# Retention, four experts and a Mish layer: product 4 ahead of product 3, and the border between the two layers re-ordered

## The chip, the cores and the metric

The kernel runs on one core of a Trainium2 chip. The metric is the device time of one execution in microseconds, as the median of several runs. Engines are named as the profile names them: PE (TensorE, matrix products), ACT (ScalarE), DVE (VectorE), POOL (GpSimd), SP (SyncE, which issues the DMAs).

## What is computed

Retention over q, k, v gives x (1152 tokens, 512 wide); four experts of width 1024 with ReLU and a weight per token follow, then one layer of width 2048 with Mish.

```python
scores = scale * np.matmul(q, k.transpose(0, 1, 3, 2))
attn = np.matmul(scores * Dmat[None], v)
x = attn.transpose(0, 2, 1, 3).reshape(1152, 512)
p = domain_probs / (domain_probs.sum(-1, keepdims=True) + 1e-09)
out = 0
for e in range(4):
    out += p[:, e:e + 1] * (np.maximum(x @ w1[e], 0.0) @ w2[e])
h = out @ w_in
g = h * np.tanh(np.log1p(np.exp(np.minimum(h, 20.0))))
return g @ w_out
```

## The kernel before, in words

**Arithmetic.** Every fp32 operand is kept as two fp32r parts, a rounded high part (made by an ACT copy) and a remainder (a subtraction on DVE or POOL). A product of two operands is three matmuls: high by remainder, high by high, remainder by high. A "product" of the first weights below is six matmuls of 512 columns (two depth blocks), all at L226.

**Units.** The hidden width of both layers is cut into 12 units of 512: units 0 to 7 belong to the four experts (NE is 8), units 8 to 11 to the Mish layer. The 1024 first tokens are multiplied with w1 by a seven-product scheme (PRODUCTS): P1 to P7 use sums of weights (key G, made on POOL at L135 to L138) and differences T1 to T4 of x. The four PSUM banks b00, b01, b10 and b11 of a call hold P1+P2, P7+P4, P5+P3 and P6. The last 128 tokens go a direct way, with x in xc.

**Steps.** `steps()` writes the order of the program as a list, and `feed_forward` emits it; every engine keeps that order. S (u, c) is `first_pair`: seven products for half c of unit u. L is `first_last`: the last tokens' product with w1 (12 matmuls, L677), turned over through DRAM (`turn_blocks`, `turn_rest`). Y (u, c, tb) is `second`: one w2 product of 24 matmuls (L693; in the Mish layer `second_t`, L709). T is the last tokens' w2 product (12 matmuls, L709). In a usual unit the order is S, L (c = 0); Y, Y (tb = 1 of the unit before); T; S, L (c = 1); Y, Y (tb = 0). Between units 7 and 8, where the result of the experts becomes the new x, it is Y, Y (tb = 0), T, Y, Y (tb = 1), S (8, 0), L (8, 1), S (8, 1).

**Inside S.** The products run as 1, 5, 7, 6, 2, 3, 4, and in the first pair of units 0 and 8 as 1, 5, 2, 3, 7, 6, 4. P1, P5 and P7 are copied out by ACT (`copy_sum`); POOL adds them into p5 (L636, L637); DVE makes p16 from P6 and P1, adds p16 to P3 and P4 and p5 to P6 (all at L622). `hidden` turns a finished bank into h: an ACT ReLU (L609) and a DVE remainder (L610), or in the Mish layer two ACT operations (L605, L606) and a DVE remainder (L607). The first two blocks of a pair's h (P2 and P4) are those for tb = 0, the others (P3 and P6) for tb = 1.

```python
            if n in (3, 6) and 3 in done and 6 in done:
                add(done[3], done[3], p16)
                add(done[6], done[6], p5)
                hidden(u, h[1][:, :, 0], done[3])
                hidden(u, h[1][:, :, 1], done[6])
```

**Lists inside S.** `early` is run behind P5, `later` behind P7: there stand weight tasks and float64 steps that were put off.

**Weights.** `weight_task` takes the next entry of a list: weight sums on POOL, or a split of a 512 KB weight tile (`split_w`: ACT copy L159, POOL remainder L163 in four pieces). A split whose tile PE still reads waits for PE.

**Float64.** The Mish layer's weights come as float64. While the experts run, each half tile goes through four stages (`STAGES`): `exponents64` (two DVE operations), `range64` (four ACT operations), `values64` (three DVE operations, then the next load, `load64`), `store64` (to DRAM). `turn64` moves each half under way by one stage per step other than S, and starts a new one at every Y of units 0 to 6 and 8.

**Border.** `new_x` splits each finished block of the experts' output into x and makes the differences T1 to T4 (L732, L742, L743; splits at L203 and L204).

Of the kernel before, what the change touches and what calls it, by code (L numbers as in the profile page):

```python
# [51 lines left out]
def steps():  # L52

    seq = [("S", 0, 0), ("L", 0, 1), ("S", 0, 1)]
    for u in range(NU):
        nxt = u + 1 < NU
        border = u == NE - 1
        seq += [("Y", u, c, 0) for c in range(2)]  # L60
        if nxt and not border:
            seq += [("S", u + 1, 0), ("L", u + 1, 0)]
        if border:
            seq.append(("T", u))
        seq += [("Y", u, c, 1) for c in range(2)]
        if not border:
            seq.append(("T", u))
        if border:
            seq += [("S", u + 1, 0), ("L", u + 1, 1), ("S", u + 1, 1)]
        elif nxt:  # L70
            seq += [("S", u + 1, 1), ("L", u + 1, 1)]
    return seq
# [7 lines left out]
def retention_moe_mish(ctx: ExitStack, tc: tile.TileContext, kq_in, kv_in, probs, w1, w2, w64, cdec, out):  # L80
# [643 lines left out]
    def new_x(c, tb, a):  # L724

        b11, b12, b21, b22 = (
            acc[:, ks, ts] for ks in (slice(0, 2), slice(2, 4)) for ts in (slice(0, TB), slice(TB, 2 * TB))
        )

        def difference(out, x, y):  # L730

            dve.tensor_tensor(out=y, in0=x, in1=y, op=ALU.subtract)  # L732
            split_x(xop[:, :, out], y, dve)

        if (c, tb) != (0, 1):
            split_x(xop[:, :, {(0, 0): B11, (1, 0): B21, (1, 1): B22}[c, tb]], a, pool)
        if (c, tb) == (0, 1):
            difference(T1, b12, b11)
        elif (c, tb) == (1, 1):
            difference(T3, b22, b12)  # L740

            dve.tensor_tensor(out=b11, in0=b22, in1=b11, op=ALU.subtract)  # L742
# [146 lines left out]
```

## Time and profile before

| what | value |
|---|---|
| runs | 659.39 us median of 3 (658.25 to 661.88) |
| the profiled execution | 661.8 us, of which the span of its instructions is 659.7 us |
| PE busy | 614.9 us (93%), 3183 matmuls |
| DVE, ACT, POOL busy | 64%, 47%, 60% |
| granted PE clock | 0.975 of 2.4 GHz on average |
| chain that ended last | PE 35%, POOL 24%, DVE 14%, ACT 12%, issue 10%, DMA 4% |

PE stands near its work for the whole span, so a stretch in which it waits is time that the kernel could lose; a wait of another engine costs only where PE waits behind it. A row of the timeline merges instructions of one kind that follow each other: start, length, line, tiles (out<-in), count, and in brackets the idle time of the engine before it with what ended it.

### The profile page before, as it was taken

Reading aid. Unit: us, or ns where it says so; the run is one execution under the profiler, and the core shown is the slowest. Engines: PE = TensorE matmul, PEld = TensorE weight load, DVE = VectorE, ACT = ScalarE, POOL = GpSimd, SP = SyncE. Lnnn points to the kernel's source line nnn. Section 1 sums busy time; section 2 is a strip of 40 time slices with the busy share of each in tenths; the row PEclk is TensorE's granted clock in tenths of the full one; section 3 lists DMA queues with packets and bytes.
Section 4 is the critical chain, followed back from the end, with each engine's and each line's share of the span. In section 5 each row is a group of like instructions: output and inputs, shape, how many; then the busy total and the mean of one; then the engine's idle time right before and its main releaser. Section 6 shows DMA issues by size and latency. Waiting matters only on the chain.

```text
span 659.7 us, 8578 instructions
## 1 busy us (share of the span) xinstructions
PE 614.9 (93%) x3183; PEld 504.4 (76%) x3183; DVE 423.6 (64%) x570; ACT 309.7 (47%) x478; POOL 395.9 (60%) x455
## 2 busy tenths in 40 slices
PE   7999999999999999999999999785769989999997
PEld 7977788788788788788787787574658868878886
DVE  2896665877887887877787787565334954244242
ACT  2665366356356346446447437213545644335130
POOL 2677849847747847747747847805951684663400
PEclk7999999999999999999999999896989989999999
DMA  8932315434424424524523523420210233121022
GB/s 332 380 102 83 107 49 155 119 125 140 144 84 144 129 95 159 139 76 136 155 97 133 159 88 104 128 64 32 61 68 2 97 86 105 35 50 43 1 64 112
DMA packets 56513, 72.30 MB, mean 110 GB/s; under 512 B 31128, under 2 KB 38296, under 8 KB 56472
## 3 DMA queue, kind: packets, MB, share of 16 engines
q1 hardware_dynamic: 56472, 71.76, 34.0%
q8 instruction: 25, 0.41, 0.2%
q14 instruction: 16, 0.13, 0.1%
HBM read 57.57 MB, written 14.17 MB: 109 GB/s over the span
## 4 chain that ended last, share of the span: by engine, by line
PE 35%; POOL 24%; DVE 14%; ACT 12%; issue 10%; DMA 4%; SPq 1%; POOLq 0%; DVEq 0%; ACTq 0%
POOL w L163 14%; PE ps L709 13%; PE b L226 11%; PE ps L693 7%; DVE b L622 3%; DVE h L610 3%; ACT h L609 3%; POOL p L636 2%; POOL p L637 2%; POOL wr L136 1%; POOL wr L137 1%; DMA O<-g 1%; POOL wr L135 1%; POOL wr L138 1%; ACT e L559 1%
## 5 line engine op out<-in xcount | busy, mean ns | idle before, releaser
L163 POOL TENSOR_TENSOR w<-wr,w 128x256 fp32r<-128x256 f32 x288 | 236.0, 851 | 154.7 <-ACT w L159 154.7
L226 PE MATMUL b<-x,w 128*128 128x512 f32 x1008 | 241.9, 397 | 4.8 <-DVE h L607 3.7
L226 PEld LDWEIGHTS b<-x,w 128*128 128x128 f32 x1008 | 188.9, 188 | 52.3 <-DVE h L607 4.5
L693 PE MATMUL ps<-h,w 128*128 128x512 f32 x768 | 179.3, 391 | 10.7 <-DVE h L610 10.7
L693 PEld LDWEIGHTS ps<-h,w 128*128 128x128 f32 x768 | 142.6, 188 | 42.9 <-DVE h L610 14.1
L709 PE MATMUL ps<-w,h 128*128 128x512 f32 x384 | 93.2, 401 | 7.2 <-ACT h L606 7.1
L709 PEld LDWEIGHTS ps<-w,h 128*128 128x128 f32 x384 | 73.3, 194 | 25.0 <-issue 8.6
L159 ACT ACTIVATE w<-wr 128x1024 fp32r<-128x1024 f32 x72 | 74.4, 1049 | 19.5 <-POOL wr L138 14.6
L238 ACT ACTIVATE p<-b 128x512 f32<-128x512 f32 x72 | 40.9, 593 | 58.4 <-PE b L226 58.3
L610 DVE SCALAR_TENSOR_TENSOR h<-b,h 128x512 fp32r<-128x512 f32 x64 | 43.4, 688 | 36.4 <-ACT h L609 35.3
L609 ACT ACTIVATE h<-b 128x512 fp32r<-128x512 f32 x64 | 38.0, 593 | 57.7 <-DVE b L622 56.6
L622 DVE TENSOR_TENSOR b<-b,p 128x512 f32<-128x512 f32 x72 | 48.5, 691 | 12.8 <-POOL p L637 12.7
L636 POOL TENSOR_TENSOR p<-p,p 128x512 f32<-128x512 f32 x24 | 31.1, 1295 | 37.5 <-ACT p L238 37.4
L607 DVE TENSOR_TENSOR h<-b,h 128x512 fp32r<-128x512 f32 x32 | 22.1, 691 | 44.7 <-ACT h L606 44.7
L677 PE MATMUL ps<-w,xc 128*128 128x256 f32 x288 | 39.1, 286 | 10.5 <-DVE xc L204 9.6
L677 PEld LDWEIGHTS ps<-w,xc 128*128 128x128 f32 x288 | 38.2, 194 | 13.2 <-issue 10.0
L558 ACT ACTIVATE e<-e,cbias 128x512 uint32<-128x512 uint32 x32 | 23.0, 720 | 52.0 <-DVE e L546 52.0
L756 DVE TENSOR_TENSOR ps<-ps,pb 128x1024 f32<-128x1024 f32 x28 | 34.3, 1226 | 15.4 <-PE ps L693 15.4
L780 DVE TENSOR_TENSOR acc<-acc,ps 128x1024 f32<-128x1024 f32 (+1 forms) x15 | 16.7, 1115 | 39.2 <-PE ps L709 39.2
L709 PE MATMUL ps<-w,hl 128*128 128x512 f32 x144 | 37.1, 410 | 4.2 <-ACT hl L609 4.2
L709 PEld LDWEIGHTS ps<-w,hl 128*128 128x128 f32 x144 | 28.4, 199 | 10.9 <-ACT hl L609 4.6
L622 DVE TENSOR_TENSOR p<-b,p 128x512 f32<-128x512 f32 x24 | 16.5, 686 | 30.0 <-PE b L226 19.0
(80 smaller groups left out, 624.3 us busy)
## 6 DMA issues: line engine op xcount, KB each, us to landing
wr<-w SPq DMA_DIRECT2D x32, 512.0 KB, 4.2
w<-w SPq DMA_DIRECT2D x32, 512.0 KB, 3.8
kq<-kq_in SPq DMA_DIRECT2D x8, 576.0 KB, 8.1
O<-g SPq DMA_DIRECT2D x16, 256.0 KB, 4.4
W<-g SPq DMA_DIRECT2D x16, 256.0 KB, 3.3
wr<-O SPq DMA_DIRECT2D x8, 512.0 KB, 3.3
wr<-W SPq DMA_DIRECT2D x8, 512.0 KB, 4.4
kv<-kv_in SPq DMA_DIRECT2D x7, 544.0 KB, 8.5
```

The source lines that it names most:

```text
L159: act.activation(out=w[:, 0], in_=t, func=AF.Copy)
L163: lo_engine.tensor_tensor(out=w[:, 1, k], in0=t[:, k], in1=f32(w[:, 0, k]), op=ALU.subtract)
L226: pe.matmul(o[t][j], w[:, a, 2 * kh + kk, fb * P:(fb + 1) * P], xop[:, b, r, kk], start=opens and kk == 0 and i == 0, stop=kk == 1 and i == 2,
L238: act.activation(out=t, in_=src, func=AF.Copy)
L609: act.activation(out=out[:, 0], in_=src, func=AF.Relu)
L610: dve.scalar_tensor_tensor(out=out[:, 1], in0=src, scalar=0.0, in1=f32(out[:, 0]), op0=ALU.max, op1=ALU.subtract)
L622: dve.tensor_tensor(out=out, in0=a, in1=b, op=ALU.add)
L636: pool.tensor_tensor(out=p5, in0=p5, in1=p7, op=ALU.add)
L677: pe.matmul(o, xc[:, b, k], w[:, a, k], start=k == 0 and n == 0, stop=k == 3 and n == 2)
L693: pe.matmul(o[:, j], w[:, a, d:d + P], h[:, b, f], start=i == f == n == 0, stop=i == f == 1 and n == 2,)
L709: pe.matmul(o[:, n], h, w[:, b, f * DM:(f + 1) * DM], start=k == f == i == 0, stop=k == f == 1 and i == 2,)
L756: dve.tensor_tensor(out=o, in0=o, in1=pbb, op=ALU.mult)
```

## The change

The order of the products in a usual S becomes 1, 5, 7, 6, 2, 4, 3, and the sums and hidden blocks of P3 and P6 are made when all seven products are done, so behind P4's. `early` becomes `behind`, a table from a product's number to what is emitted behind it. In the first pairs of units 0 and 8 the last tokens' product stands behind P2 instead of P5. At the border, T stands between the last two Y; T1 is made right behind it, and the differences for T3 and T2 are taken behind P1 ahead of the split of xc, the rest (`last_t`) behind P5. New float64 halves start at L and at the Y of c = 0 (not in unit 7), the weight task of a step stands ahead of its float64 stages, the last Y of unit 7 has none, and the Y of unit 8 have two. The float64 tiles have five buffers instead of four. The first load of q and k is issued as two halves, by SP and by ACT. `cbias` has 16 columns instead of 3.

```diff
     for u in range(NU):
...
+        y = [[("Y", u, c, tb) for c in range(2)] for tb in range(2)]
+        t = [("T", u)]
+        if u == NE - 1:
+            seq += y[0] + y[1][:1] + t + y[1][1:] + [("S", u + 1, 0), ("L", u + 1, 1), ("S", u + 1, 1)]
...
-    cbias = keep.tile([P, 3], F32, tag="cbias", name="cbias")
+    cbias = keep.tile([P, 16], F32, tag="cbias", name="cbias")
...
-            sp.dma_start(out=kq, in_=kq_in[b, pr])
+            if u == 0:
+                sp.dma_start(out=kr, in_=kq_in[b, pr, :, 0])
+                act.dma_start(out=qr, in_=kq_in[b, pr, :, 1])
+            else:
+                sp.dma_start(out=kq, in_=kq_in[b, pr])
...
-            if n in (3, 6) and 3 in done and 6 in done:
+            for f in behind.get(n, ()):
+                f()
+            if len(done) == 7:
                 add(done[3], done[3], p16)
                 add(done[6], done[6], p5)
...
+    def last_x():
+
+        x_split(B22, b22, pool)
+        x_minus(b12, b22, b12)
+        x_minus(b11, b22, b11)
+        split_x(xc, acc_last, dve)
+
+    def last_t():
+        x_split(T3, b12)
+        x_minus(b21, b21, b11)
+        x_split(T2, b11)
+        x_split(T4, b21)
...
                 turn_rest(acc_last)
+                x_minus(b11, b12, b11)
+                x_split(T1, b11)
...
-                if (u, c) == (NE, 0):
-                    early.insert(0, lambda: split_x(xc, acc_last, dve))
-                if (u, c) in ((0, 0), (NE, 0)):
-                    early.append(lambda: first_last(u, 0))
+                late = (u, c) in ((0, 0), (NE, 0))
+                behind = {}
+                if late:
+                    behind[2] = [lambda: first_last(u, 0)]
+                    behind[5] = early if u == 0 else [last_t]
+                if (u, c) == (NE, 0):
+                    behind[1] = [last_x]
...
-                first_pair(u, c, early, later, (1, 5, 2, 3, 7, 6, 4) if late else (1, 5, 7, 6, 2, 3, 4))
+                first_pair(u, c, behind, later, (1, 5, 2, 3, 7, 6, 4) if late else (1, 5, 7, 6, 2, 4, 3))
...
+            if m != "S" and (m, u, *at) != ("Y", NE - 1, 1, 1):
+                task(2 if u in (0, NE) and m == "Y" else 1)
             if m != "S":
-                turn64(m == "Y" and u != NE - 1, later.append if ahead else lambda f: f())
+                new = (m, *at) in (("L", 0), ("L", 1), ("Y", 0, 0), ("Y", 0, 1)) and not i_x <= i <= i_x + 7 and i > 2
+                turn64(new, later.append if ahead else lambda f: f())
...
-            if m != "S":
-                task(2 if u == 0 and m == "Y" else 1)
```

In the changed file the lines from L198 on stand at most 8 away from those of before: L620 and L608 there are L622 and L610 here, L603 and L604 are L605 and L606, L153 is L159, L232 is L238, L198 is L204, L755, L756 and L769 are L756, L757 and L770, L660 is L662.

DVE at unit 2, c = 1 (S (2, 1)), before: b00 is P2's bank, b01 P4's, b10 P3's, b11 P6's.

```order
L622 TENSOR_TENSOR p16_1661<-b11_1616,p1_1625 128x512
L610 SCALAR_TENSOR_TENSOR h_1617<-b00_1613,h_1617 128x512
L622 TENSOR_TENSOR b10_1615<-b10_1615,p16_1661 128x512
L622 TENSOR_TENSOR b11_1616<-b11_1616,p5_1633 128x512
L610 SCALAR_TENSOR_TENSOR h_1618<-b10_1615,h_1618 128x512
L610 SCALAR_TENSOR_TENSOR h_1618<-b11_1616,h_1618 128x512
L622 TENSOR_TENSOR b01_1614<-b01_1614,p16_1661 128x512
L610 SCALAR_TENSOR_TENSOR h_1617<-b01_1614,h_1617 128x512
```

And now:

```order
L620 TENSOR_TENSOR p16_1656<-b11_1615,p1_1624 128x512
L608 SCALAR_TENSOR_TENSOR h_1616<-b00_1612,h_1616 128x512
L620 TENSOR_TENSOR b01_1613<-b01_1613,p16_1656 128x512
L608 SCALAR_TENSOR_TENSOR h_1616<-b01_1613,h_1616 128x512
L620 TENSOR_TENSOR b10_1614<-b10_1614,p16_1656 128x512
L620 TENSOR_TENSOR b11_1615<-b11_1615,p5_1632 128x512
L608 SCALAR_TENSOR_TENSOR h_1617<-b10_1614,h_1617 128x512
L608 SCALAR_TENSOR_TENSOR h_1617<-b11_1615,h_1617 128x512
```

P4's sum and remainder (b01) moved from the end to the third and fourth place, ahead of the two sums of P3 and P6, of which the latter reads POOL's p5.

DVE between units 7 and 8, before, from the turning over of the last tokens on (acc holds the experts' output, x and xc are the new operands, ps is a w2 product):

```order
L662 STREAM_TRANSPOSE hs_697<-acc_87 128x128 x4
L756 TENSOR_TENSOR ps_3848<-ps_3848,pb_3314 128x1024
L757 TENSOR_TENSOR acc_87<-acc_87,ps_3848 128x2x512
L732 TENSOR_TENSOR acc_87<-acc_87 128x2x512
L204 TENSOR_TENSOR x_84<-acc_87,x_84 128x1024
L756 TENSOR_TENSOR ps_3878<-ps_3878,pb_3314 128x1024
L757 TENSOR_TENSOR acc_87<-acc_87,ps_3878 128x2x512
L732 TENSOR_TENSOR acc_87<-acc_87 128x2x512
L204 TENSOR_TENSOR x_84<-acc_87,x_84 128x1024
L742 TENSOR_TENSOR acc_87<-acc_87 128x2x512
L743 TENSOR_TENSOR acc_87<-acc_87 128x2x512
L204 TENSOR_TENSOR xc_85<-acc_87,xc_85 128x512
```

And now, from the last tokens' sum on:

```order
L769 SCALAR_TENSOR_TENSOR acc_87<-ps_3853,pl_86,acc_87 128x4x128
L660 STREAM_TRANSPOSE hs_698<-acc_87 128x128 x4
L727 TENSOR_TENSOR acc_87<-acc_87 128x2x512
L198 TENSOR_TENSOR x_84<-acc_87,x_84 128x1024
L755 TENSOR_TENSOR ps_3879<-ps_3879,pb_3309 128x1024
L756 TENSOR_TENSOR acc_87<-acc_87,ps_3879 128x2x512
L727 TENSOR_TENSOR acc_87<-acc_87 128x2x512 x2
L198 TENSOR_TENSOR xc_85<-acc_87,xc_85 128x512
L198 TENSOR_TENSOR x_84<-acc_87,x_84 128x1024
L727 TENSOR_TENSOR acc_87<-acc_87 128x2x512
```

The last tokens' sum and turning over stand ahead of the last w2 product's sums instead of ahead of two products' sums; T1's difference and remainder follow them, and xc's remainder has one x remainder ahead of it instead of two.

ACT from unit 8's first pair into its second, before (w is a weight copy, p1, p5 and p7 the copied products):

```order
L605 ACTIVATE b10_3920<-b10_3920 128x512
L606 ACTIVATE h_3923<-b10_3920 128x512
L605 ACTIVATE b11_3921<-b11_3921 128x512
L606 ACTIVATE h_3923<-b11_3921 128x512
L605 ACTIVATE b01_3919<-b01_3919 128x512
L606 ACTIVATE h_3922<-b01_3919 128x512
L238 ACTIVATE p1_4062<-b00_4050 128x512
L238 ACTIVATE p5_4070<-b10_4052 128x512
L238 ACTIVATE p7_4078<-b01_4051 128x512
L159 ACTIVATE w_4082<-wr_3846 128x1024
L159 ACTIVATE w_4088<-wr_4023 128x1024
L605 ACTIVATE b00_4050<-b00_4050 128x512
```

And now:

```order
L603 ACTIVATE b01_3907<-b01_3907 128x512
L604 ACTIVATE h_3910<-b01_3907 128x512
L603 ACTIVATE b10_3908<-b10_3908 128x512
L604 ACTIVATE h_3911<-b10_3908 128x512
L603 ACTIVATE b11_3909<-b11_3909 128x512
L604 ACTIVATE h_3911<-b11_3909 128x512
L153 ACTIVATE w_4039<-wr_3823 128x1024
L232 ACTIVATE p1_4059<-b00_4047 128x512
L232 ACTIVATE p5_4067<-b10_4049 128x512
L232 ACTIVATE p7_4075<-b01_4048 128x512
L603 ACTIVATE b00_4047<-b00_4047 128x512
L604 ACTIVATE h_4051<-b00_4047 128x512
```

P4's bank (b01) is first of the three; the two weight copies between p7 and the first Mish of the second pair are gone, and one stands ahead of p1.

## Rows read from the trace of the kernel before

**Rows 1.** Waits of all engines: engine, line, releaser: us in total, times, longest.
```profile
PE ps L693 <- DVE h L610: 10.7, 8, 1.6
...
DVE e L546 <- DMA w<-w: 6.0, 6, 2.6
```

**Rows 2.** PE timeline, units 2 and 3: start us, us, engine, line, [idle before].
```profile
163.72 3.57 PE L693 MATMUL ps<-h,w 128*128 128x512 f32 x15
168.80 7.78 PE L693 MATMUL ps<-h,w 128*128 128x512 f32 x33 [1.51 <-DVE h L610]
176.42 9.96 PE L226 MATMUL b<-x,w 128*128 128x512 f32 x42
...
187.62 11.05 PE L693 MATMUL ps<-h,w 128*128 128x512 f32 x48
198.51 2.88 PE L709 MATMUL ps<-w,hl 128*128 128x512 f32 x12
```

**Rows 3.** DVE timeline at unit 2, c = 1: the sums and remainders.
```profile
164.73 0.70 DVE L622 TENSOR_TENSOR b<-b,p 128x512 f32<-128x512 f32 x1 [1.81 <-POOL p L637]
...
166.70 0.69 DVE L622 TENSOR_TENSOR b<-b,p 128x512 f32<-128x512 f32 x1
168.06 0.69 DVE L610 SCALAR_TENSOR_TENSOR h<-b,h 128x512 fp32r<-128x512 f32 x1 [0.66 <-ACT h L609]
```

**Rows 4.** PE timeline, unit 7 to unit 9.
```profile
412.25 7.77 PE L693 MATMUL ps<-h,w 128*128 128x512 f32 x33 [1.62 <-DVE h L610]
424.21 5.41 PE L709 MATMUL ps<-w,hl 128*128 128x512 f32 x12 [4.19 <-ACT hl L609]
...
452.90 2.90 PE L677 MATMUL ps<-w,xc 128*128 128x256 f32 x12 [9.57 <-DVE xc L204]
...
463.11 1.57 PE L677 MATMUL ps<-w,xc 128*128 128x256 f32 x12
...
471.39 7.27 PE L226 MATMUL b<-x,w 128*128 128x512 f32 x30 [2.02 <-DVE h L607]
478.50 3.65 PE L709 MATMUL ps<-w,h 128*128 128x512 f32 x15
487.29 9.36 PE L709 MATMUL ps<-w,h 128*128 128x512 f32 x33 [5.13 <-ACT h L606]
...
538.01 9.52 PE L709 MATMUL ps<-w,h 128*128 128x512 f32 x33 [1.94 <-ACT h L606]
```

**Rows 5.** DVE timeline between unit 7 and unit 8.
```profile
429.65 0.75 DVE L770 SCALAR_TENSOR_TENSOR acc<-ps,pl,acc 128x512 f32<-128x512 f32 x1 [4.66 <-PE ps L709]
430.44 0.89 DVE L662 STREAM_TRANSPOSE hs<-acc 128x128 f32<-128x128 f32 x4
...
437.71 1.23 DVE L732 TENSOR_TENSOR acc<-acc 128x1024 f32<-128x1024 f32 x1
...
446.07 2.22 DVE L204 TENSOR_TENSOR x<-acc,x 128x1024 fp32r<-128x1024 f32 x1 [1.12 <-ACT x L203]
...
451.54 1.21 DVE L204 TENSOR_TENSOR xc<-acc,xc 128x512 fp32r<-128x512 f32 x1
```

**Rows 6.** ACT timeline, unit 7 and unit 8.
```profile
438.97 1.06 ACT L203 ACTIVATE x<-acc 128x1024 fp32r<-128x1024 f32 x1 [13.43 <-DVE acc L732]
...
463.52 2.00 ACT L159 ACTIVATE w<-wr 128x1024 fp32r<-128x1024 f32 x2
...
466.33 0.60 ACT L606 ACTIVATE h<-b 128x512 fp32r<-128x512 f32 x1
...
478.70 1.06 ACT L159 ACTIVATE w<-wr 128x1024 fp32r<-128x1024 f32 x1 [4.05 <-PE b L226]
```

**Rows 7.** POOL timeline between unit 7 and unit 8.
```profile
444.86 2.35 POOL L204 TENSOR_TENSOR x<-acc,x 128x1024 fp32r<-128x1024 f32 x1 [14.87 <-ACT x L203]
```

**Rows 8.** Stretch 424 to 426 us: engines' busy us, granted PEclk, DMA share, GB/s.
```profile
424.00:426.00 2.00, 1.79 (x4) 1.34 (x5) 0.81 (x1) 1.21 (x2) 2.00 (x2) 0.50 0.64 254
```

**Rows 9.** SP's queue at the start.
```profile
0.74 0.38 SPq L289 DMA_DIRECT2D kq<-kq_in  x1
```

More of the change, by code (lines that the diff above doesn't have):

```diff
@@ L57, in steps @@
     for u in range(NU):
[L58 to L71, printed above, removed]
+        y = [[("Y", u, c, tb) for c in range(2)] for tb in range(2)]
+        t = [("T", u)]
+        if u == NE - 1:
+            seq += y[0] + y[1][:1] + t + y[1][1:] + [("S", u + 1, 0), ("L", u + 1, 1), ("S", u + 1, 1)]
+        elif u + 1 < NU:
+            seq += y[0] + [("S", u + 1, 0), ("L", u + 1, 0)] + y[1] + t + [("S", u + 1, 1), ("L", u + 1, 1)]
+        else:
+            seq += y[0] + y[1] + t
     return seq
@@ L543, in exponents64 @@
         hi_w = raw64[i][:, :, :, 1]
-        g = ph.tile([P, 2, 256], F32, tag="g", name="g64", bufs=4)
-        e = ph.tile([P, 2, 256], U32, tag="g", name="e64", bufs=4)
+        e = ph.tile([P, 2, 256], U32, tag="g", name="e64", bufs=5)
+        g = ph.tile([P, 2, 256], F32, tag="g", name="g64", bufs=5)
         dve.tensor_scalar(
@@ L612, in hidden, with first_pair @@
         )
-    def first_pair(u, c, early, later, order):
+    def first_pair(u, c, behind, later, order):
         pre = ahead_of.pop((u, c), None)
@@ L722, in load_pb, with x_minus, x_split @@
             pb_t[e, tb] = pb
[L724 to L742, printed above, removed]
-            dve.tensor_tensor(out=b21, in0=b21, in1=b11, op=ALU.subtract)
-            early.append(lambda: (split_x(xop[:, :, T2], b11, dve), split_x(xop[:, :, T4], b21, dve)))
+    b11, b12, b21, b22 = (
+        acc[:, ks, ts] for ks in (slice(0, 2), slice(2, 4)) for ts in (slice(0, TB), slice(TB, 2 * TB))
+    )
+    def x_minus(out, x, y):
+        dve.tensor_tensor(out=out, in0=x, in1=y, op=ALU.subtract)
+    def x_split(n, t, lo_engine=dve):
+        split_x(xop[:, :, n], t, lo_engine)
+    def last_x():
[8 more added lines that the diff above has]
+        x_split(T4, b21)
     acc_last = acc[:, :, NTB * TB:]
@@ L757, in m2 @@
             dve.tensor_tensor(out=a, in0=a, in1=o, op=ALU.add)
-            if u == NE - 1:
-                new_x(c, tb, a)
+            if u == NE - 1 and tb == 0:
+                x_split(B21 if c else B11, a, pool)
             return
@@ L790, in feed_forward @@
         pbs = []
+        i_x = seq.index(("Y", NE - 1, 0, 0))
         for i, (m, u, *at) in enumerate(seq):
```

4 lines of the change are left out of this document (1 added, 3 removed).

## The prediction

> **What bounds the kernel now.** Read the list of waits first: TensorE (PE) is busy for nearly the whole span, so what can be won is what it waits for, and one line leads that list: the w2 products of L693 wait eight times for a remainder written by DVE, 10.7 us in all [rows 1]. The PE timeline shows the place. In unit 2 the first 15 matmuls of a pair of w2 products run, then PE stands still for 1.51 us before the other 33; the next pair of w2 products in the same unit runs its 48 matmuls in one piece [rows 2]. The 16th matmul is the first to read the second block of h of c = 1, the one that product 4 makes. The DVE timeline says why it is late: P3's branch comes first, its sum with p5 waits until 164.73 for POOL, and P4's sum (166.70) and remainder (168.06) stand behind it in DVE's order [rows 3]. The same PE view from unit 7 to unit 9 shows the rest: 4.19 us for the last tokens' hidden values, 9.57 us for their x, 2.02 us for a PSUM bank, and 5.13 and 1.94 us at the first w2 product of units 8 and 9 [rows 4].
>
> **P4 ahead of P3, units 0 to 7.** PE's work stays; only its order changes, and DVE's. P4 now ends one product earlier and its sum and remainder stand ahead of P3's branch, so POOL's p5 no longer holds them. The ScalarE (ACT) queue of this step also loses a float64 range step. After P4, PE still has P3, the last tokens' L677 and 15 matmuls to do, 1.4 + 1.4 + 3.4 = 6.2 us: a seventh of 9.96, the 1.57 of an L677 and the 3.57 of 15 matmuls, each row less the 0.16 by which it overlaps the next (187.62 + 11.05 against 198.51) [rows 2, 4]. The chain behind P4 is a sum 0.69, an ACT step 0.60, a remainder 0.69 [rows 3, 6]: 2.0 us. I take the wait as gone at all eight places. A wait also costs a refill: 176.42 − 163.72 = 12.70 with it, 198.51 − 187.62 = 10.89 without, so 1.81 for a wait of 1.51 [rows 2]. Gain: 10.7 + 8 × 0.30 = **13.1**.
>
> **Units 8 and 9.** Here hidden is Mish, two ACT steps. In unit 8, ACT also stood 4.05 us on a weight copy that waits for PE's own products to free the tile (478.70) [rows 6]; the change places that copy after the products. With P4 first, its chain is 0.69 + 1.2 + 0.69 = 2.6 us against 1.4 + 3.4 = 4.8 on PE. Both waits go, with the slow stretch behind each: after them 33 matmuls took 9.36 and 9.52, against 7.77 in unit 7 [rows 4]. Gain 5.13 + 1.59 + 0.30 and 1.94 + 1.75 + 0.30: **11.0**.
>
> **The border, unit 7 to 8.** From the end of the waited pair (412.25 + 7.77 = 420.02) to the second L677 (463.11) PE needs 43.1 us [rows 4]. Without a wait its work is a pair of w2 products 10.9, the last tokens' w2 2.7, seven products 9.8 and an L677 1.4: 24.8 [rows 2]. What stays of the 18.3 I work out from the end of the last w2 product (time 0) in the new DVE order. The last tokens' w2 now ends at −5.4; DVE is held until about −3.3 by the float64 step and the sums ahead of it (an estimate: three operations and four sums of some 1.2). Then 0.75 and 0.89 (accumulate, turn over), the T1 difference 1.23, its ACT half 1.06, its remainder 1.23 [rows 5, 6]: T1 is ready at +1.9, 0.6 after P5 could start. Two sums of the last product follow (2 × 1.23, +4.4), then the differences b12 (+5.6) and b11, then xc's remainder. For b11 the rows give two prices: 1.23 with POOL idle, 2.22 beside POOL's 2.35 remainder [rows 5, 7]; POOL's B22 remainder lies just there, so I take 2.2, and 1.2 for xc: +9.0. PE reaches its L677 at 0.6 + 3 × 1.4 = +4.9 and waits 4.1, instead of 9.57. Behind it T3, T2 and T4 come at 1.2 to 2.4 us apart, no slower than the products that read them. By the Trainium skill, SBUF — State Buffer, section "Who interferes with whom", a DVE operation with two SBUF inputs and a GpSimd one that reads SBUF exclude each other for a whole instruction; by that alone b11 would take 2.35 + 1.23 and the wait be 5.5.
>
> A wait of that size also costs clock: after the 4.19 us the granted clock was 0.50, the 1.2 GHz level [rows 8], and 12 matmuls took 5.41 instead of 2.88; the waits of 1.94 and 5.13 us cost 1.75 and 1.6 [rows 2, 4]. I take 1.8 here, and 0.3 in case the hidden values of the last tokens are just late. Gain: 18.3 − 0.6 − 4.1 − 1.8 − 0.3 = **11.5**. Bounds: 9 (no more of the wait than half goes) to 15.
>
> **What it gives back.** In the first pair of unit 8 the change now finishes P4 before it sums P3 and P6, while the pair behind it reuses P3's bank as its second product. ACT's two weight copies end at 465.5 [rows 6]; then 1.2 (Mish, copy), 0.69 (remainder), 0.69 (P3's sum, behind it on DVE), 1.2 and 0.69: the bank is free near 470.1, and six products of 1.4 end at 478.5, where they end now [rows 4]. Even, but PE now waits in one piece of 4.2 us rather than 1.6 and 2.02, and pays the clock once: **−1.8**. Unit 0 has the same pair with single ACT steps; I take 0 there, between ±1.
>
> **A larger cbias.** The built program shows one more effect: every later tile moves by 32 bytes. x now starts at a multiple of 64 bytes of a partition (16,576, was 16,544), and w, h, hl and acc, which did, now lie 32 off. The matmuls that stream x take (9.96 − 0.16)/42 = 233 ns, those that stream h (11.05 − 0.16)/48 = 227 [rows 2]. If the offset of the streamed operand is what costs 6.5 ns, the 24 pairs' 1008 x matmuls gain 6.6, the 768 that stream h and the 528 that stream w lose 8.4, and 288 half-width ones lose 0.9: **−2.8**. It is the only difference I find between these rows. Bounds: +6.6 (only x matters) to −9.3.
>
> **At nothing.** Splitting the first kq load over two queues saves SP a part of one issue of 0.38 [rows 9]; the bytes ahead of the first k and v stay the same, so 0, ±0.4. The Trainium skill, DMA: Bandwidth & Descriptors, section "Issuing engines are not separate DMA queues", says that only issue time is saved; no run here shows it. The re-placed float64 steps and the fifth buffer hide under PE; if that cover goes, each late one costs what the slower rival below prices.
>
> **Sum.** 13.1 + 11.0 + 11.5 − 1.8 − 2.8 = 31.0. The profiled execution took 661.8, so 630.8 against it; it lies 2.4 above the median of the runs, 659.39, so I forecast 628.4.
>
> **Rivals.**
> - Lighter: neither wait takes the clock (3.6 back) and the offset costs nothing (2.8 back): 622. For it: the 2.02 us wait left 30 matmuls at 7.27, nearly full speed [rows 4]. Against: 1.94 did not.
> - POOL first: the exclusion named above holds b11 for the full instruction, 1.4 more: 629.8. Row 446.07 shows half of it.
> - The last tokens' way through DRAM: their w2 now ends one product (5.4 us) later, and xc's ACT half waits for that transfer rather than for DVE. If it lands 4 us after DVE is ready: 632.4. Against: DVE alone needs 9.0 us.
> - The weights take over at the eight waits: POOL's remainder of the second w2 half ends last. Then 10 of the 13.1 stay: 638. Against: ACT loses a step there, so POOL starts earlier.
> - Slower: DVE held by a float64 load. In the new placing one exponent step per unit reads a load issued one step before. DVE waited for such loads six times, 2.6 us at most [rows 1]. Behind it stands the sum that frees a PSUM tile; PE has 5.4 us of other product, less 2.5 for the two sums, so some 3 us are free. From 3 us on each us costs PE one, in seven units: to lose 31.0 + 3.3 the load must be 3 + 34.3/7 = 8 us late, giving 663.
>
> **How the numbers follow.** Forecast 0.64 (its own range 624 to 634), lighter 0.14, POOL first 0.08, DRAM 0.05, weights 0.06, slower 0.03. A measurement tells 0.5%, 3.3 us, from no change. All cases but the last lie below 656; I leave 0.02 for a case between: faster 0.95, same 0.02, slower 0.03. The range 619 to 638 takes in the lighter case with a little of the x-only gain, and the weights case at its upper end; it leaves out some 0.15.
>
> **What would show it.** The L693 wait for DVE gone from the list, and pairs of w2 products in one row of 48 in every unit; no wait at 5.13's and 1.94's places; an L677 wait of 3 to 6 us at the border; one new wait of about 4 us for P5 in unit 8's second pair; L226 rows of 42 at 9.7 and rows of 48 at 11.4. I am wrong if a w2 wait stays, if PE waits for w or ps in the units, or if the rows of 48 stay at 11.05.

## The result and the profile after

| | kernel before | changed kernel |
|---|---|---|
| median, lowest to highest of 4 runs each | 659.32 (658.25 to 661.88) | 636.12 (634.86 to 636.99) |
| the profiled execution, its span | 661.8, 659.7 | 635.8, 633.7 |
| PE busy, granted clock | 614.9 (93%), 0.975 | 608.8 (96%), 0.984 |

The ratio is 0.9641, with a 95% interval of 0.9609 to 0.9674: faster by 23.2 us, to 636.1, where 31.0 and 628.4 were forecast. The two spans differ by 26.0. Lines of the changed kernel: L220 are the products (L226 before), L691 and L707 the w2 products (L693, L709), L675 the last tokens (L677), L198 the remainders of x (L204), L605 and L608 those of h (L607, L610), L755 and L756 the two operations that add a w2 product to acc.

PE's rows in the list of waits of the changed kernel (us in total, times, longest):

```profile
PE b L220 <- ACT p L232: 4.4, 3, 2.6
PE b L220 <- DVE h L605: 4.3, 1, 4.3
PE ps L675 <- DVE xc L198: 3.6, 1, 3.6
PE ps L691 <- DVE acc L756: 3.3, 1, 3.3
```

The eight waits that led the list [rows 1] are gone. Of the four rows that lead it now, the forecast had two: 4.3 for P3's bank in unit 8 and 3.6 for xc. The 3.3 for acc and the 2.6 for ACT's copy p are new. The PE timeline of the changed kernel shows where they lie (start, length, what was done, wait before):

```profile
113.40 11.09 PE L691 MATMUL ps<-h,w 128*128 128x512 f32 x48
124.33 9.96 PE L220 MATMUL b<-x,w 128*128 128x512 f32 x42
...
394.88 16.49 PE L691 MATMUL ps<-h,w 128*128 128x512 f32 x72
...
412.71 2.57 PE L707 MATMUL ps<-w,hl 128*128 128x512 f32 x10 [0.89 <-DVE hl L608]
418.62 7.31 PE L691 MATMUL ps<-h,w 128*128 128x512 f32 x24 [3.35 <-DVE acc L756]
425.77 4.37 PE L220 MATMUL b<-x,w 128*128 128x512 f32 x18
433.76 2.90 PE L675 MATMUL ps<-w,xc 128*128 128x256 f32 x12 [3.62 <-DVE xc L198]
436.45 7.03 PE L220 MATMUL b<-x,w 128*128 128x512 f32 x24
443.32 1.57 PE L675 MATMUL ps<-w,xc 128*128 128x256 f32 x12
...
450.57 11.26 PE L220 MATMUL b<-x,w 128*128 128x512 f32 x36 [4.28 <-DVE h L605]
461.67 11.05 PE L707 MATMUL ps<-w,h 128*128 128x512 f32 x48
...
505.82 4.46 PE L220 MATMUL b<-x,w 128*128 128x512 f32 x18 [2.62 <-ACT p L232]
511.53 11.09 PE L707 MATMUL ps<-w,h 128*128 128x512 f32 x48
```

Outside the border every pair of w2 products now runs in one piece, in units 8 and 9 too, where it broke before [rows 2, 4]. The 42 x matmuls of a pair still take 9.96 and the 48 still 11.05.

From such rows the span can be cut into stages, each from the start of one row to the start of the next (us). Run e9 is the kernel before with P4 ahead of P3 and nothing else, e10 the best arrangement that was found; both follow below.

| stage | before | changed | e9 | e10 |
|---|---|---|---|---|
| to the first product P1 | 40.36 | 38.57 | 37.76 | 37.18 |
| to the first w2 product | 26.87 | 27.36 | 27.30 | 27.57 |
| units 0 to 7, to the end of unit 7's first two w2 products | 352.63 | 339.84 | 339.54 | 339.84 |
| border, to the second L of unit 8 | 43.25 | 37.55 | 43.51 | 28.56 |
| to unit 8's first w2 product | 15.39 | 18.35 | 16.93 | 11.91 |
| unit 8's first w2 pair | 17.99 | 10.89 | 11.50 | 10.89 |
| to unit 9's first w2 product | 36.01 | 38.97 | 36.01 | 36.01 |
| unit 9's first w2 pair | 14.87 | 10.92 | 11.54 | 10.89 |
| to the last product | 105.74 | 104.69 | 104.69 | 104.71 |

The product order won what was forecast: 12.8 in units 0 to 7, 7.1 + 3.95 in the pairs of units 8 and 9. The border won 5.7 of its 11.5; unit 8 gave back 3.0, and unit 9 gave back 3.0 that were not forecast.

DVE's timeline of the changed kernel shows what happened at the border:

```profile
410.10 2.55 DVE L608 SCALAR_TENSOR_TENSOR hl<-hs,hl 128x512 fp32r<-128x512 f32 x1 [1.65 <-ACT hl L607]
412.58 1.22 DVE L564 SCALAR_TENSOR_TENSOR e<-w,e 128x512 uint32<-128x512 uint32 x1
...
414.98 1.10 DVE L570 TENSOR_TENSOR g<-g,e 128x512 f32<-128x512 f32 x1
416.00 1.22 DVE L755 TENSOR_TENSOR ps<-ps,pb 128x1024 f32<-128x1024 f32 x1
417.26 1.22 DVE L756 TENSOR_TENSOR acc<-acc,ps 128x1024 f32<-128x1024 f32 x1
...
430.78 2.83 DVE L198 TENSOR_TENSOR xc<-acc,xc 128x512 fp32r<-128x512 f32 x1
```

and POOL's timeline of the same kernel what ran beside it, there and in unit 8:

```profile
409.72 2.39 POOL L198 TENSOR_TENSOR x<-acc,x 128x1024 fp32r<-128x1024 f32 x1
...
429.63 3.43 POOL L198 TENSOR_TENSOR x<-acc,x 128x1024 fp32r<-128x1024 f32 x1 [12.97 <-ACT x L197]
...
488.61 7.75 POOL L157 TENSOR_TENSOR w<-wr,w 128x256 fp32r<-128x256 f32 x8 [8.31 <-ACT w L153]
```

The 72 w2 matmuls end at 411.4, but the sum of their third product waits behind hl's remainder and behind the three value operations of a float64 half, and ends at 418.5. The last w2 product, one small T product later, needs the PSUM tile that this sum frees. The hl remainder, 0.81 before, took 2.55 and ended 0.54 after POOL's operation (412.65 against 412.11). xc's took 2.83 and ended 0.55 after POOL's (433.61 against 433.06).

The windows of the changed kernel (length, busy us of PE, PEld, DVE, ACT and POOL, granted PE clock, DMA share, GB/s) show what a wait costs on top:

```profile
433.70:436.40 2.70, 2.64 (x12) 2.67 (x13) 2.70 (x3) 0.49 (x1) 0.00 (x0) 0.50 0.00 0
450.60:456.00 5.40, 5.40 (x13) 4.25 (x14) 1.05 (x2) 2.34 (x4) 2.79 (x4) 0.50 0.33 49
456.00:461.70 5.70, 5.70 (x26) 4.57 (x25) 1.99 (x3) 1.83 (x4) 4.69 (x5) 0.97 0.40 138
```

Behind the waits of 3.62 and 4.28 the granted clock stood at its 1.2 GHz level (0.50): 13 matmuls in 5.4 us, then 26 in 5.7.

### The profile page after: what moved, and what is told of

Read it like the earlier page. It is cut to its first block, busy times and chain, and to the rows that moved or that the text cites. A ratio compares the mean times of both kernels' runs of the same rounds, so it can differ in the third digit from the quotient of the medians.

```text
span 633.7 us, 8597 instructions
## 1 busy us (share of the span) xinstructions
PE 608.8 (96%) x3183; PEld 504.5 (80%) x3183; DVE 432.9 (68%) x570; ACT 312.7 (49%) x478; POOL 401.9 (63%) x455
## 4 chain that ended last, share of the span: by engine, by line
PE 73%; DVE 8%; POOL 8%; DMA 3%; ACT 3%; issue 3%; DVEq 0%; POOLq 0%
PE b L220 29%; PE ps L691 24%; PE ps L707 16%; POOL w L157 5%; PE ps L675 4%; DMA cst_sb<-cdec 3%; DVE acc L260 1%; DVE x L266 1%; DVE x L416 1%; ACT w L153 1%; POOL p L633 1%; POOL p L632 1%; DVE acc L756 1%; DVE ps L755 1%; POOL wr L132 1%
## 5 line engine op out<-in xcount | busy, mean ns | idle before, releaser
L220 PE MATMUL b<-x,w 128*128 128x512 f32 x1008 | 245.0, 401 | 10.2 <-ACT p L232 4.4
L220 PEld LDWEIGHTS b<-x,w 128*128 128x128 f32 x1008 | 191.8, 191 | 58.0 <-ACT p L232 5.8
L691 PE MATMUL ps<-h,w 128*128 128x512 f32 x768 | 178.6, 392 | 3.3 <-DVE acc L756 3.3
L691 PEld LDWEIGHTS ps<-h,w 128*128 128x128 f32 x768 | 144.3, 189 | 33.1 <-issue 3.7
L153 ACT ACTIVATE w<-wr 128x1024 fp32r<-128x1024 f32 x72 | 75.0, 1052 | 28.2 <-POOL wr L132 27.5
L707 PE MATMUL ps<-w,h 128*128 128x512 f32 x384 | 88.3, 390 | 0.0
L707 PEld LDWEIGHTS ps<-w,h 128*128 128x128 f32 x384 | 71.7, 188 | 14.6
L232 ACT ACTIVATE p<-b 128x512 f32<-128x512 f32 x72 | 42.4, 596 | 69.8 <-PE b L220 69.6
L607 ACT ACTIVATE h<-b 128x512 fp32r<-128x512 f32 x64 | 38.1, 596 | 53.0 <-DVE b L620 44.3
L608 DVE SCALAR_TENSOR_TENSOR h<-b,h 128x512 fp32r<-128x512 f32 x64 | 42.7, 688 | 25.5 <-ACT h L607 24.5
L632 POOL TENSOR_TENSOR p<-p,p 128x512 f32<-128x512 f32 x24 | 35.9, 1494 | 36.4 <-ACT p L232 36.4
L755 DVE TENSOR_TENSOR ps<-ps,pb 128x1024 f32<-128x1024 f32 x28 | 34.4, 1230 | 31.7 <-PE ps L691 31.7
L620 DVE TENSOR_TENSOR b<-b,p 128x512 f32<-128x512 f32 x72 | 47.5, 691 | 0.6
L605 DVE TENSOR_TENSOR h<-b,h 128x512 fp32r<-128x512 f32 x32 | 22.1, 692 | 37.4 <-ACT h L604 37.4
L675 PEld LDWEIGHTS ps<-w,xc 128*128 128x128 f32 x288 | 38.2, 194 | 6.1 <-issue 4.0
L675 PE MATMUL ps<-w,xc 128*128 128x256 f32 x288 | 38.9, 286 | 3.6 <-DVE xc L198 3.6
L620 DVE TENSOR_TENSOR p<-b,p 128x512 f32<-128x512 f32 x24 | 16.5, 686 | 32.4 <-PE b L220 15.6
L570 DVE TENSOR_TENSOR g<-g,e 128x512 f32<-128x512 f32 x32 | 35.3, 1103 | 1.1
L707 PE MATMUL ps<-w,hl 128*128 128x512 f32 x144 | 35.0, 391 | 0.9 <-DVE hl L608 0.9
```

The source lines that it names most:

```text
L153: act.activation(out=w[:, 0], in_=t, func=AF.Copy)
L220: pe.matmul(o[t][j], w[:, a, 2 * kh + kk, fb * P:(fb + 1) * P], xop[:, b, r, kk], start=opens and kk == 0 and i == 0, stop=kk == 1 and i == 2,
L232: act.activation(out=t, in_=src, func=AF.Copy)
L607: act.activation(out=out[:, 0], in_=src, func=AF.Relu)
L608: dve.scalar_tensor_tensor(out=out[:, 1], in0=src, scalar=0.0, in1=f32(out[:, 0]), op0=ALU.max, op1=ALU.subtract)
L620: dve.tensor_tensor(out=out, in0=a, in1=b, op=ALU.add)
```

## The experiments

Each is one edit of the changed kernel, unless it is said otherwise. Three rounds each (e12 five), all beside the kernel before on the same chip. Runs of different chips are compared by their ratios, and by the places in their traces. The changed kernel's ratio is 0.9641; e1 and e2, which turned out to change nothing, lie at 0.9622 and 0.9619.

**e9: the product order alone** (edit of the kernel before).

```diff
-first_pair(u, c, early, later, (1, 5, 2, 3, 7, 6, 4) if late else (1, 5, 7, 6, 2, 3, 4))
+first_pair(u, c, early, later, (1, 5, 2, 3, 7, 6, 4) if late else (1, 5, 7, 6, 2, 4, 3))
```

> The kernel before with one edit: P4 ahead of P3 in all pairs but the first ones of units 0 and 8. Theory that the order alone takes the eight waits (step 'P4 ahead of P3'): all pairs of w2 products of units 0 to 7 in one row of 48, 12.8 saved, and unit 9's wait of 1.94 with its slow stretch, 4.0; unit 8's wait of 5.13 stays for the most part, since ACT's copy of weights that waits for PE stands ahead of P4's hidden values there: about 642.5. Rival, the order takes unit 8's wait as well: 7.0 more, 635.5. Rival, the waits need the re-placed float64 steps too: half or more of the eight stay, 649 or above.

635.14 us, ratio 0.9622 (0.9599 to 0.9644): the whole gain, within what can be measured. The second theory held: the order takes unit 8's wait as well. PE's two longest waits in this run, unit 8's first pair of w2 products, and one row of ACT:

```profile
PE ps L677 <- DVE xc L204: 9.6, 1, 9.6
PE ps L709 <- ACT hl L609: 4.2, 1, 4.2
```

```profile
465.04 11.65 PE L709 MATMUL ps<-w,h 128*128 128x512 f32 x48
```

```profile
463.84 1.06 ACT L159 ACTIVATE w<-wr 128x1024 fp32r<-128x1024 f32 x1 [3.07 <-PE b L226]
```

ACT still stands on the weight copy, for 3.07 us; but behind it P4's hidden values come as the second of four, ahead of P3's, and P4's remainder is written by 469.3 (DVE), 4.3 us after the pair's start; a stall of 0.6 is left in its row (11.65 for 48, where 11.05 is usual). So the re-placed copy of the forecast's step was hardly needed. All else in the change, border, weights and float64 steps together, is worth 2.5 us (the two columns' sums without the first stage: 588.57 against 591.02), and no difference shows between the runs. By the table it won 6.0 at the border and 1.2 in the pairs of units 8 and 9, and lost 1.4 ahead of unit 8's pair and 3.0 ahead of unit 9's.

**e1: the kq load in one piece.**

```diff
-            if u == 0:
-                sp.dma_start(out=kr, in_=kq_in[b, pr, :, 0])
-                act.dma_start(out=qr, in_=kq_in[b, pr, :, 1])
-            else:
-                sp.dma_start(out=kq, in_=kq_in[b, pr])
+            sp.dma_start(out=kq, in_=kq_in[b, pr])
```

> The changed kernel with the first kq in one load on SP again. My step 'At nothing' took the split as 0 +-0.4; in the changed kernel the first product P1 starts at 38.57 instead of 40.36. Theory that the split does this: P1 starts near 40.4 again, PE waits over 2 us for the first kv, and the time is 1.8 up, about 637.9. Rival, that the start differs from one execution to the next or for another reason: P1 stays near 38.6 and the time within 0.6 of 636.1.

635.83 us, ratio 0.9622 (0.9599 to 0.9644). P1 starts at 38.68 without the split and at 38.57 with it: nothing. Over the 14 profiles of this study P1 starts between 37.10 and 40.36, and the profiled execution of the kernel before has the latest of them. Up to P1, e9 is the kernel before unchanged, and starts P1 at 37.76; so the 1.8 us of the first stage are a chance of the execution. In the execution before, PE waited 2.4 us for a kv load; in e9's, no wait of that size shows.

**e2: the small cbias.**

```diff
-    cbias = keep.tile([P, 16], F32, tag="cbias", name="cbias")
+    cbias = keep.tile([P, 3], F32, tag="cbias", name="cbias")
```

> The changed kernel with cbias 3 wide again, so that x, w, h and the rest lie where they lay before. My step 'A larger cbias' took 233 against 227 ns as the offset of the streamed operand; the changed kernel's rows stayed at 9.96 for 42 and 11.05 for 48. Theory that the offset plays no part: these rows stay at 9.96 and 11.05 once more, time 636.1 within 0.6. Rival, that the offset counts and something else in the change hid it: rows of 42 or of 48 move by more than 0.1, and the time by 2 or more.

635.62 us, ratio 0.9619 (0.9584 to 0.9654). The offset plays no part: with either, 42 x matmuls take 9.96 and 48 w2 matmuls 11.05, as in unit 0 of this run:

```profile
65.26 11.05 PE L691 MATMUL ps<-h,w 128*128 128x512 f32 x48
```

**e3: the float64 half away from the border.**

```diff
-... and not i_x <= i <= i_x + 7 and i > 2
+... and not i_x - 1 <= i <= i_x + 7 and i > 2
```

> The changed kernel, but the float64 half that begins at the last-token product of unit 7's second pair begins some steps later, so that its three value operations no longer stand on DVE ahead of the sums of Y(7,0,1). Theory of the PSUM tile: those 3.5 us are why the last w2 product waits 3.35 us for a free ps tile, and the wait costs clock too (24 matmuls in 7.31 instead of 5.45). Without them the wait is under 0.4, the 24 take about 5.5, and 5 us are saved: 631. Rival, hl: DVE is held by the hl remainder of 2.55 us all the same, a wait of 1.5 or more stays, 633 to 634. Rival, given back: the L675 wait for xc (3.62) grows by what is won, time within 1 of 636.

629.5 us, ratio 0.9526 (0.9506 to 0.9545). The wait for the PSUM tile is gone, and the last w2 product starts as soon as T ends:

```profile
414.27 5.72 PE L691 MATMUL ps<-h,w 128*128 128x512 f32 x24
```

From the 72 matmuls' start to the end of this product it is 26.02 (419.99 − 393.97), against 31.05 (425.93 − 394.88) in the changed kernel: 5.0, as expected. The waits of 0.9, 3.6 and 4.3 stay as they were. So the tile's wait is the value operations' doing, not hl's.

**e4: B21's remainder on DVE.**

```diff
-                x_split(B21 if c else B11, a, pool)
+                x_split(B21 if c else B11, a, dve if c else pool)
```

> The changed kernel with the remainder of B21, the second x block at the border, on DVE instead of POOL. In the changed kernel the remainder of the last tokens' hidden values (hl) takes 2.55 us on DVE beside POOL's B21 remainder of 2.39, where it took 0.81 in the kernel before with POOL idle. Theory that the two exclude each other: hl takes about 0.8 again, the 0.89 wait for it nearly goes, the wait for a ps tile shrinks by about 1, about 1 us saved: 635. Rival, hl is slow for another reason: it stays above 2 us. Rival, DVE's extra 1.2 us cancels it: hl fast, but time within 0.6 of 636.1.

633.27 us, ratio 0.9584 (0.955 to 0.9617). DVE's hl row and PE's row of the last w2 product:

```profile
410.25 0.68 DVE L608 SCALAR_TENSOR_TENSOR hl<-hs,hl 128x512 fp32r<-128x512 f32 x1
```

```profile
416.91 7.20 PE L691 MATMUL ps<-h,w 128*128 128x512 f32 x24 [3.33 <-DVE acc L756]
```

With POOL not in its way hl takes 0.68 instead of 2.55, and the wait of 0.89 is gone. The wait for the tile did not shrink, since T itself came 0.9 earlier. From the 72 matmuls to the last w2 product: 22.54, was 23.74; 1.2 saved at the place, too little for the runs to tell (the intervals of e4, e1 and the changed kernel overlap).

**e5: xc first.**

```diff
     def last_x():
+        split_x(xc, acc_last, dve)
         x_split(B22, b22, pool)
         x_minus(b12, b22, b12)
         x_minus(b11, b22, b11)
-        split_x(xc, acc_last, dve)
```

> The changed kernel with the last tokens' xc split ahead of B22's split and of the differences b12 and b11, on ACT and on DVE. In the changed kernel xc's remainder on DVE takes 2.83 us beside POOL's B22 remainder of 3.43 and ends at 433.6; PE waits 3.62 for it. Theory that DVE's order and the company of POOL set this: xc is ready near 429.5, the wait at L675 goes, about 0.4 to 1.8 us of it comes back at P3, which needs POOL's B22; with the clock, 2 to 4 us are saved: 632 to 634. Rival, the last tokens' way through DRAM sets it: the wait stays above 2.5 and only changes its name, time within 1 of 636. Rival, B22 on POOL is next: P3 waits 3 us or more, no gain.

631.67 us, ratio 0.9572 (0.9544 to 0.96). DVE's rows, POOL's and one of PE's:

```profile
428.60 0.69 DVE L198 TENSOR_TENSOR xc<-acc,xc 128x512 fp32r<-128x512 f32 x1
429.20 4.54 DVE L727 TENSOR_TENSOR acc<-acc 128x1024 f32<-128x1024 f32 x2
```

```profile
429.71 2.95 POOL L198 TENSOR_TENSOR x<-acc,x 128x1024 fp32r<-128x1024 f32 x1 [12.78 <-ACT x L197]
```

```profile
432.71 1.65 PE L220 MATMUL b<-x,w 128*128 128x512 f32 x6 [1.10 <-POOL x L198]
```

xc's remainder takes 0.69 and the wait of 3.62 is gone; 1.10, 0.56 and 0.61 come back at P3, P7 and P6. From P1 to the second L: 14.26, was 17.55. The way through DRAM did not set this wait. What POOL held up before now hits the differences: two of them take 4.54, against 2.36 in the changed kernel.

**e6 and e7: unit 8's first pair.** e6 brings back the old place of the sums of P3 and P6; e7 also puts the two weight copies behind the pair.

```diff
-            if len(done) == 7:
+            if n in (3, 6) and 3 in done and 6 in done:
```

> The changed kernel, but in the first pairs of units 0 and 8 the sums and hidden values of P3 and P6 come as soon as both are done, ahead of P4, as in the kernel before. Theory that the order of the sums is a part of unit 8's new wait of 4.28 (ACT's two weight copies stand ahead of both orders): P3's hidden values come right behind the copies, P5 waits about 1.8, then P7 about 0.9 for P4's bank: 1.5 saved and up to 2.5 of clock, 632 to 634.6. Rival, only the copies count: the wait stays above 3.5 and the time within 1 of 636. Rival, P4 late costs the w2 products: a wait at L707 behind the pair, slower than 636.

> As e6, and unit 8's two weight copies stand behind all four hidden values of that first pair. Theory: ACT has 2.0 us less ahead of P3's hidden values, P5 finds its bank free, P7 waits under 1 us, and the slow clock behind the wait goes as well (36 matmuls in about 8.6 instead of 11.26): 3.5 + 2.5 saved against the changed kernel, 630. Rival, the first w2 product waits for the weights that now come later: 2 us or more at L707, 634 or above.

e6: 632.59 us, ratio 0.9592 (0.9561 to 0.9623); e7: 634.85, ratio 0.9621 (0.9589 to 0.9654). PE's rows, two of e6 and the second of e7:

```profile
447.49 1.67 PE L220 MATMUL b<-x,w 128*128 128x512 f32 x6 [1.64 <-DVE h L605]
451.18 7.26 PE L220 MATMUL b<-x,w 128*128 128x512 f32 x30 [2.03 <-DVE h L605]
```

```profile
451.41 8.80 PE L220 MATMUL b<-x,w 128*128 128x512 f32 x30 [2.02 <-DVE h L605]
```

With the old place of the sums the two waits are 3.67 together, not much less than 4.28; of the 3.0 that e6 saves up to the first w2 product (15.39, was 18.35) most is clock. The waits of e7, 1.65 and 2.02, are the same as e6's, so the weight copies were not on the chain; e7's theory fell. The changed kernel's own trace says so too: ACT is done with the two copies at 445.75, and then still waits for DVE's sum before P4's Mish.

```profile
446.01 0.58 ACT L603 ACTIVATE b<-b 128x512 f32<-128x512 f32 x1 [0.27 <-DVE b L620]
```

The rows of e7 show what was on it: ACT loads Mish's table only behind P7's copy, and DVE's p16 stands behind the remainder of P2's hidden values.

```profile
441.13 1.28 ACT L603 ACT_TABLE_LOAD   x1
```

```profile
443.67 0.69 DVE L605 TENSOR_TENSOR h<-b,h 128x512 fp32r<-128x512 f32 x1 [5.18 <-ACT h L604]
444.28 0.68 DVE L620 TENSOR_TENSOR p<-b,p 128x512 f32<-128x512 f32 x1
```

The two runs also differ by 1.5 us behind equal waits: granted clock 1.00 in e6 (451.2 to 455), 0.66 in e7 (451.4 to 455).

**e11: the pair arranged anew.** After e7: Mish of P2 right behind P2, ahead of T2 and T4; the sums of P3, P6 and P4 one behind the other, then the hidden values of P3, P6, P4.

```diff
+            elif n == 2 and 7 not in done and u == NE:
+                hidden_act(u, h[0][:, :, 0], done[n])
...
                 add(p16, done[n], p1)
+                if 3 in done:
+                    add(done[3], done[3], p16)
+                    add(done[6], done[6], p5)
...
                 add(done[n], done[n], p16)
-                hidden(u, h[0][:, :, 1], done[n])
+                if 3 not in done:
+                    hidden(u, h[0][:, :, 1], done[n])
...
-                    behind[5] = early if u == 0 else [last_t]
+                    behind[5] = early if u == 0 else [first_t]
...
+                    behind[2].insert(0, last_t)
```

> The changed kernel with the first pair of unit 8 (and the sums of unit 0's) arranged anew: Mish of P2 runs right behind P2 on ACT, before T2 and T4 are split, the sums of P3, P6 and P4 come one behind the other on DVE, then the hidden values of P3, P6, P4. Run e7 showed that the weight copies were not what held P3's bank (1.65 + 2.02 with them behind); theory now is the chain P7's copy, Mish table load 1.28, P2's hidden values and remainder, only then DVE's sums. Taken out of it, P5 waits under 0.8 and P7 under 0.8, against 4.28, and the slow clock goes with them: 3 to 6 saved, 630 to 633. Rival, ACT's Mish steps alone set it: waits of 2.5 or more stay in all. Rival, the earlier Mish delays T2 or T4: a new wait of 1 us or more for x ahead of P6 or P4.

629.56 us, ratio 0.9523 (0.9493 to 0.9554). PE's row behind P1 and P5:

```profile
446.35 7.27 PE L220 MATMUL b<-x,w 128*128 128x512 f32 x30 [0.23 <-DVE h L605]
```

0.23 in place of 4.28, and full clock: from the second L to unit 8's first w2 product 11.73, was 18.35. This is 6.6, more than expected. Two things changed at once, the place of Mish's table load and of P2's hidden values, and the order of the sums. By e6 the old order of the sums alone leaves 3.67 of waits; the first alone was not run.

**e8: float64 halves 28 to 31 in unit 9.**

```diff
-... and not i_x <= i <= i_x + 7 and i > 2
+... and not i_x <= i <= i_x + 15 and i > 2
```

> The changed kernel, but float64 halves 28 to 31 begin in unit 9's steps instead of unit 8's. In the changed kernel PE waits 2.62 us in S(9,1) for ACT's copy of P1, behind a weight copy that waits for POOL's sums; POOL took 7.75 for 8 remainders and 4.15 for 4 sums just there, beside DVE's float64 steps, against 5.5 and 3.0 elsewhere. Theory that this company slows POOL by 3 us and so makes the wait: 8 remainders in 5.7, sums in 3.0, the wait of 2.62 gone, 2.9 saved: 633. Rival, the two weight tasks in one step put POOL behind in any case: a wait of 1.5 or more stays. Rival, the same turns up one unit later: a new wait in unit 10, time within 1 of 636.

631.69 us, ratio 0.9564 (0.9529 to 0.9599). POOL's row and PE's:

```profile
487.37 5.61 POOL L157 TENSOR_TENSOR w<-wr,w 128x256 fp32r<-128x256 f32 x8 [7.98 <-ACT w L153]
```

```profile
496.47 9.96 PE L220 MATMUL b<-x,w 128*128 128x512 f32 x42
```

The eight remainders take 5.61, not 7.75; ACT's split behind POOL's sums starts 0.2 us before the pair (496.28), where it started 3.2 behind (500.64 against 497.44), P1's copy comes in time, and the pair runs in one row. So the float64 halves of unit 8 made the wait of 2.62. They did it on two engines: beside DVE's steps POOL was slow, and ACT's rows of the changed kernel show four of their range operations, 2.7 us, between the late split and the copies of P1, P5 and P7.

```profile
500.64 1.06 ACT L153 ACTIVATE w<-wr 128x1024 fp32r<-128x1024 f32 x1 [5.43 <-POOL wr L132]
501.61 0.71 ACT L556 ACTIVATE e<-e,cbias 128x512 uint32<-128x512 uint32 x1
...
503.73 0.61 ACT L559 ACTIVATE g<-g 128x512 f32<-128x512 uint32 x1
...
505.20 1.55 ACT L232 ACTIVATE p<-b 128x512 f32<-128x512 f32 x3
```

e8 took both away. By an estimate from these rows either one alone would have left next to no wait: PE is done with its first 24 matmuls at 503.2, and P1's copy would have ended near 503.1 without the range operations, and near 501.4 with the split 4.4 us earlier.

**e10: all of it.** The edits of e3, e4, e5, e8 and e11.

> The changed kernel with the edits of e3, e4, e5, e8 and e11 together (float64 halves away from the border and from unit 8, B21's remainder on DVE, xc first, the new first pair). By the sum of the places: 5.0 (ps wait and its clock) + 0.9 (hl) + 3.3 (xc) + 2.9 (S(9,1)) + 5 (unit 8's pair) = 17 against 636.1: 619. Rival, the gains overlap, since each removed wait exposes the next (P3's wait for POOL's B22, T2, T4): 622 to 626. Rival, float64 halves moved to unit 9 come late for unit 11's weights: a wait for w in unit 10 or 11, above 628.

616.15 us (615.65 to 616.2), ratio 0.9319 (0.9284 to 0.9355): faster than both kernels, some 20 us below the changed one. The granted clock is 0.997. The places add up to 18.4, where 17 were expected: 9.0 at the border, 6.4 to unit 8's first w2 product, 3.0 to unit 9's (the table of stages). Leading rows of PE's waits in this run (the 2.0 lies in unit 0's first pair, the other two rows in unit 8's):

```profile
PE b L220 <- ACT p L232: 2.3, 2, 2.0
PE b L220 <- POOL x L198: 1.6, 1, 1.6
...
PE b L220 <- DVE x L198: 1.2, 2, 0.6
```

**e12: B22's remainder on DVE as well**, on top of e10.

```diff
         split_x(xc, acc_last, dve)
-        x_split(B22, b22, pool)
+        act.activation(out=xop[:, :, B22][:, 0], in_=b22, func=AF.Copy)
         x_minus(b12, b22, b12)
-        x_minus(b11, b22, b11)
+        dve.tensor_tensor(out=xop[:, :, B22][:, 1], in0=b22, in1=f32(xop[:, :, B22][:, 0]), op=ALU.subtract)
...
         x_split(T3, b12)
+        x_minus(b11, b22, b11)
```

> As e10, with B22's remainder on DVE instead of POOL, between the differences b12 and b11 (b11 comes behind T3). In e10 POOL's B22 remainder takes 3.05 us and DVE's two differences beside it 4.52 (2.36 elsewhere): P3 waits 1.58 for it, P7 and P6 0.55 and 0.60. Theory that they hold each other up: with POOL idle the two differences take 1.2 each, P3 waits under 0.8, the three waits together fall from 2.7 to about 1.8, 1 us saved at this place: 615. Rival, DVE's added 1.2 us only moves the waits to P6 and P4: 2.7 or more in all, 616 or above.

615.42 us, ratio 0.9319 (0.9297 to 0.934). With POOL idle each difference takes 1.2 and P3 waits 0.62, but P6 now waits 1.62: 2.2 in all, was 2.7. At the place 0.8 is saved (9.77 from the first to the second L, was 10.53), too little for the runs to tell.

## Why the prediction was right, and where its sizes were not

The direction, the main cause and the range held; e9 shows the cause. The size was off, and that the range held is in part luck. 636.1 lies above the forecast's own range of 624 to 634, and inside 619 to 638 only because that reached up to the price of a rival, "the weights take over", which did not happen. Two of the forecast's own signs of being wrong came true: the rows of 48 stayed at 11.05, and PE waits for a PSUM tile, if only at the border. Against the spans (26.0 won, 31.0 forecast), step by step:

- **P4 ahead of P3, units 0 to 7** (13.1): 12.8. The wait and the refill of 0.30 per place were sized right. The remainder of the second w2 half did not come late anywhere: the rival "the weights take over" did not happen.
- **Units 8 and 9** (11.0): 11.05. Right in size. The reason given for unit 8, the re-placed copy, was half wrong: e9 leaves the copy where it was and has 6.5 of the 7.1 there.
- **The border** (11.5): 5.7. The L675 wait came as forecast (3.62 for 4.1), and T1 was in time. The step that failed is "DVE is held until about −3.3 by the float64 step and the sums ahead of it". It counted this delay for T1 alone. But one of those sums frees the PSUM tile of the last w2 product, which after the change stands only one T product behind instead of a full product: a wait of 3.35, and 24 matmuls in 7.31 instead of 5.7 behind it. (The rival "slower" has this sum in mind for the usual units; the border was not looked at in this way.) e3 took the float64 step away and got 5.0 of the missing 5.8. The hidden values of the last tokens, put at 0.3, cost 0.9 (e4), and the clock after the xc wait some 2.6 instead of 1.8 (2.90 for 1.56, 7.03 for 5.76).
- **What it gives back** (−1.8): −3.0. The one wait of 4.2 came as 4.28; the clock behind it cost 2.7 (36 matmuls in 11.26, was 8.55 at full speed) instead of 1.8. Its cause was not ACT's two copies, as the step said: with them moved (e7) the waits stayed. They went with e11, which takes Mish's table load and P2's hidden values out of the chain and puts the sums together; its two parts were not run apart. Unit 0, taken as 0 ±1, lost 0.5, but e9, whose first pair in unit 0 is that of the kernel before, lost 0.4 there too.
- **A larger cbias** (−2.8): 0. The step "if the offset of the streamed operand is what costs 6.5 ns" was wrong (e2). The only difference that was found between two rows was taken for its cause; it should have stayed a bound. Why matmuls of x take 233 ns and those of h 227 is still open.
- **At nothing**: the kq split is 0, as said (e1). By the Trainium skill, DMA: Bandwidth & Descriptors, section "Issuing engines are not separate DMA queues", a second queue saves only issue time; no run here can show so little, since the start varies by more between executions. The re-placed float64 steps were not free: besides the border they cost 2.96 in unit 8, where they slowed POOL and stood ahead of P1's copy on ACT (e8). The sentence that they "hide under PE" left out whom they hold up on the other engines.

So the forecast of the gain was 2.8 too low for cbias, and 5.8 + 1.2 + 3.0 too high for the border, unit 8 and unit 9. The execution's earlier start (1.8) and 1.0 in units 10 and 11 made the gap in the spans smaller, 5.0. The forecast did not count the latter; it belongs to the product order, since e9 has it too: there 48 matmuls took 11.57 and 96 took 22.46 before, and 11.05 and 21.93 in both. Against the medians the gap is 7.7: the forecast took 2.4 off because the profiled execution before lay that far above its median, while the changed kernel's lay 0.3 below its own.

Of the rivals, "Lighter" failed, since all three waits over 3 us took the clock; only its other half, that the offset costs nothing, came true. "POOL first" had the right rule and the wrong operation: xc's remainder, not b11, stood behind POOL. Its text says that "Row 446.07 shows half of it" [rows 5]; the row shows the whole: that remainder started when POOL's instruction [rows 7] was half done, and ended 1.08 behind its end (448.29 against 447.21), about the 1.23 that it takes alone. The way through DRAM and a float64 load that holds DVE did not show in the changed kernel; in e10, with the rest out of the way, ACT waits 0.32 for the former. No experiment put the border's new order into a kernel without P4 ahead of P3.

## What to carry to other kernels

When work is moved past a rotating PSUM tile, ask who frees the tile and what stands ahead of that operation on its engine: an off-path step that was harmless behind a long product is on the path behind a short one. A plain swap in the order of two products won as much as the whole change; test such a part alone first. And a cheap step on DVE has a second price, paid by POOL and by whoever waits for POOL.
